# Reordering the loads and the early batches of a fused attention and gated-MLP kernel

## The chip, the cores and the metric

The kernel runs on one core of one Trainium2 chip. The metric is device time in microseconds (us). TensorE (PE) does matrix products, VectorE (DVE) and ScalarE (ACT) elementwise work, GpSimd (POOL) copies and the loads that cast, SyncE (SP) the output writes and the transposes done by DMA. Each engine runs its own instructions in program order and waits on semaphores for the others.

## The reference

Eight batches of eight heads, 576 positions, head size 64. A first attention packs k and v into 32 rows with p as queries; a second lets q attend to these 32 rows. The result, 4608 rows of 512, goes through a layer with h * cos(h) between two products.

```python
p_packed = sm_attn(p, k, v)            # p: 8 x 8 x 32 x 64
out = sm_attn(q, p_packed, p_packed)   # softmax with scale 1/8
x = out.transpose(0, 2, 1, 3).reshape(4608, 512)
h = x @ w_in                           # w_in: 512 x 2048
return (h * cos(h)) @ w_out            # w_out: 2048 x 512
```

Inputs and output are float32; the kernel computes in bf16 and accumulates in float32.

## The kernel before

**One batch** goes through these steps, each a helper function:

- `load(n, b)` brings k, q or v of a batch to SBUF with a cast to bf16, issued from POOL. `permute_v` rearranges v, on POOL or VectorE.
- k and q are transposed either by `pe_T` (24 PE transposes in three groups of eight, each group with one copy out of PSUM, L101 and L76) or by `xbar` (one DMA transpose on SP's queue, L92).
- `s1` (L123, L132): scores of p against k, and two exps on ScalarE into the tile a1. `recips`: reciprocals of its sums. a1 is transposed by `a1_pe` (12 PE transposes, two copies) or `a1_xbar` (DMA).
- `pp` (L162): the packed rows, copied out as ppT by two copies on VectorE and two on ScalarE.
- `ppw(b, n)` (L181): ppT times quarter n of w_in, giving PPW, with one cast out of PSUM by VectorE or ScalarE. The second attention is folded in this way, so that x is never formed.
- `s2` (L189): scores of q and two exps into a2u. `sums2` (L197, L199): sums over each head's 32 rows, and their logarithm. `normalise` (L205, L207): exp of the negated logarithm, and two VectorE instructions into a2n.
- `h_mm(b, fc)` for 16 chunks fc of 128 columns: four matmuls PPW by a2n (L220), the cosine on ScalarE (L224), the product h * cos(h) on VectorE into gT (L227), and a copy of the odd 64 rows into the tile joint on POOL (L231).
- `out_gen(b)`: gT times w_out (L270), 16 matmuls for each chunk c of 128 rows, a copy of the result to osb by VectorE or ScalarE in turn, and its write by SP. With 4 or 5 chunks a batch has 64 or 80 output matmuls.

**The order is written by hand.** `out_gen` is a generator; `fill(n)` puts the next n output matmuls of the batch before into TensorE's stream wherever it stands. So while slot s computes h of batch s, the output of batch s-1 fills TensorE. `set_filler` first uses up what is left and then starts on the next batch. `slot(s, ...)` runs the 16 chunks of `h_mm`, spreading the fillers evenly, with `pp`, `ppw`, `pack_p` and others put in at given chunks. What runs between two slots, from `ACT.preload_act_table_set` (ScalarE's table for exp and log; the cosine needs another) to `normalise`, is called the head of a slot here.

**Buffers.** TensorE writes to three PSUM tiles psA that are used strictly in turn: an allocation waits until whatever used the same buffer three allocations ago was read. Output matmuls have two tiles of their own (ot). There is one buffer each for kbf, qbf, vbf, kT and qT, so a load waits for the transpose of the batch before; v permuted has two.

**Start.** Batch 0 is handled with little to overlap, with `warm` matmuls on zeros in the gaps. Its cosine phase has no output to fill TensorE with. Loads stand in POOL's queue in this order: k, v, q of batch 0, the four quarters of w_in with the rest of p between, the four quarters of w_out, then k, v, q of batches 1 and 2.

```python
    set_filler(0)
    ACT.preload_act_table_set(EXP_SET)
    fill(4)
    pe_T("k", 1)
    fill(3)
    s1(1)
    permute_v(1, V)
    fill(8)
    a1_pe(1)
```

In the head of slot 1, 43 of batch 0's 64 output matmuls are placed, along with all of batch 1's attention and with k and s1 of batch 2.

Of the kernel before, what the change touches and what calls it, by code (L numbers as in the profile page):

```python
# [8 lines left out]
FP32 = mybir.dt.float32  # L9
# [6 lines left out]
def kernel(  # L16
# [55 lines left out]
    def copy(eng, out, in_):  # L72
        if eng is ACT:
            ACT.copy(out=out, in_=in_)  # L74
        else:
            eng.tensor_copy(out=out, in_=in_)  # L76
# [2 lines left out]
        return A.tile([128, 2, 512 if dt == FP32 else 1024], dt, name="psA", tag="A")  # L79

    def load(n, b):
        bf[n, b] = bf_pool.tile([TP, H, C * D], BF16, name=n + "bf", tag=n + "bf")
        G.dma_start(out=bf[n, b], in_=srcs[n][b].rearrange("h (p c) d -> p h (c d)", c=C))  # L83

    def permute_v(b, eng=G):
        vp[b] = vp_pool.tile([TP, C, H * D], BF16, name="vp", tag="vp")
        copy(eng, vp[b].rearrange("p c (h d) -> p c h d", h=H),
             bf["v", b].rearrange("p h (c d) -> p c h d", c=C))

    def xbar(n, b):  # L90
        t = xT[n, b] = att_pool.tile([128, H * 3, TP], BF16, name=n + "T", tag=n + "T")
        nc.sync.dma_start_transpose(out=t, in_=bf[n, b].rearrange("p h x -> p (h x)"))  # L92

    def pe_T(n, b, engs=(V, V, V)):
        t = xT[n, b] = att_pool.tile([128, H * 3, TP], BF16, name=n + "T", tag=n + "T")
        flat = bf[n, b].rearrange("p h x -> p (h x)")
        for i in range(3):
            ps = psa(BF16)
            for j in range(8):
                o = 8 * i + j  # L100
                nc.tensor.transpose(ps[:, 0, j * TP:(j + 1) * TP], flat[:, o * 128:(o + 1) * 128],  # L101
                                    ident[0:TP, 0:TP])
            copy(engs[i], t[:, 8 * i:8 * i + 8].rearrange("p a x -> p (a x)"),
                 ps[:, 0, 0:8 * TP])
# [69 lines left out]
    def ppw(b, n, eng=None):  # L174
        if b not in PPW:
            PPW[b] = ppw_pool.tile([128, 2, DF], BF16, name="PPW", tag="PPW")
        ps = psa()
        for x in range(4):
            for y in range(2):
                r = slice(64 * y, 64 * y + 64)  # L180
                nc.tensor.matmul(ps[32 * x:32 * x + 32, y, :], ppT[b % 2][r, 2 * x + y, :],  # L181
                                 w_in_bf[r, x, n * 512:(n + 1) * 512], start=True, stop=True)
        copy(eng or (V, ACT)[n % 2], PPW[b][:, :, n * 512:(n + 1) * 512], ps)

    def s2(b):
        a2u[b] = att_pool.tile([128, 2, S], BF16, name="a2u", tag="a2u")
        ps = scores(ppT[b % 2], xT["q", b])
        for y in range(2):
            ACT.activation(out=a2u[b][:, y].rearrange("p (e x) -> p e x", e=2),  # L189
                           in_=ps[y][:, :, 0:HS], func=AF.Exp, scale=rs1[b][:, y:y + 1])  # L190
# [46 lines left out]
    def pieces_of(b, c):  # L237
        ob = out[b * S:(b + 1) * S, :].rearrange("(p c) d -> c p d", c=C)
        if c == 4:
            o0 = out[(b - 1) * S:b * S, :].rearrange("(p c) d -> c p d", c=C)  # L240
            return [(0, 64, o0[5, 32:96]), (64, 128, ob[5, 32:96])]
        res, z = [], c * 128
        while z < c * 128 + 128:
            j, p0 = z // TP, z % TP
            n = min(TP - p0, c * 128 + 128 - z)
            res.append((z - c * 128, z - c * 128 + n, ob[2 * (j % 3) + j // 3, p0:p0 + n]))
            z += n
        return res

    def n_chunks(b):  # L250
        return 5 if b % 2 and b < B - 1 else 4
# [11 lines left out]
                q.dma_start(out=rows[:, cols], in_=osb[a:z, cols])  # L263

    def out_gen(b):
        for c in range(n_chunks(b)):
            ps = O.tile([128, DM], FP32, name="ot", tag="ot")
            for fc in range(NFC):
                w = joint[b // 2][:, fc, :] if c == 4 else gT[b][:, fc, c * 128:(c + 1) * 128]
                nc.tensor.matmul(ps, w, w_out_bf[:, fc, :], start=(fc == 0), stop=(fc == NFC - 1))  # L270
                if fc < NFC - 1:
                    yield
            osb = o_pool.tile([128, DM], FP32, name="osb")
            copy((V, ACT)[n_out[0] % 2], osb, ps)
            n_out[0] += 1
            for a, z, rows in pieces_of(b, c):
                nc.sync.dma_start(out=rows, in_=osb[a:z, :])
            yield

    filler = [None, 0]  # L280

    def set_filler(b):
        fill(1000)
        filler[0] = out_gen(b)
        filler[1] = 16 * n_chunks(b)
# [7 lines left out]
    def load_w_in(n):  # L293
        G.dma_start(out=w_in_bf[:, :, n * 512:(n + 1) * 512],
                    in_=moe_w_in.rearrange("(a p) n -> p a n", p=128)[:, :, n * 512:(n + 1) * 512])

    def load_w_out(n):
        G.dma_start(out=w_out_bf[:, n * 4:(n + 1) * 4, :],
                    in_=moe_w_out.rearrange("(a p) n -> p a n", p=128)[:, n * 4:(n + 1) * 4, :])

    def dup_p(a, b):
        for t in range(2):
            V.tensor_copy(out=p_bf[:, a:b, t, :], in_=p_raw[:, a:b, :])

    def warm(n):
        for _ in range(n):
            nc.tensor.matmul(wps, wz[:, 0:128], wz, start=True, stop=True)
# [3 lines left out]
    load("v", 0)  # L311
    make_identity(nc, ident)
    load("q", 0)
    load_w_in(0)
    load_w_in(1)
    G.dma_start(out=p_raw[:, 2:, :], in_=p_rows[:, 2:, :])
    load_w_in(2)
    load_w_in(3)
    for n in range(4):
        load_w_out(n)  # L320
    load("k", 1)
    load("v", 1)
    load("q", 1)
    load("k", 2)
    load("v", 2)
    load("q", 2)
    wz = const.tile([128, 512], BF16, name="wz")
    wps = O.tile([128, 512], FP32, name="wps", tag="ot")
    V.memset(wz, 0.0)
# [5 lines left out]
        V.memset(t[:, :, :, TP:128], 0.0)  # L335

    warm(7)
    dup_p(0, 2)
    pack_p(0, 1)
    warm(9)  # L340
    pe_T("k", 0, (V, ACT, V))
    s1(0)
    permute_v(0, V)
    warm(3)
    a1_pe(0)
    recips(0)
    pp(0)
    pe_T("q", 0, (V, ACT, V))
    s2(0)
    ppw(0, 0)  # L350
    sums2(0, 0)
    sums2(0, 1)
    normalise(0)
    warm(6)
    dup_p(2, 16)
    for fc in range(NFC):
        h_mm(0, fc)()
        if fc in (1, 4, 7):
            ppw(0, 1 + fc // 3)
        if fc == 10:  # L360
            pack_p(1, 3)

    set_filler(0)
    ACT.preload_act_table_set(EXP_SET)
    fill(4)
    pe_T("k", 1)
    fill(3)
    s1(1)
    permute_v(1, V)
    fill(8)  # L370
    a1_pe(1)
    recips(1)
    fill(4)
    pp(1)
    pe_T("q", 1)
    fill(3)
    ppw(1, 0)
    s2(1)
    fill(4)
    pe_T("k", 2)  # L380
    ppw(1, 1)
    fill(3)
    s1(2)
    fill(4)
    sums2(1, 0)
    fill(4)
    sums2(1, 1)
    normalise(1)
    fill(6)
    a1_pe(2)  # L390
    recips(2)
    load("k", 3)

    def slot(s, pieces, hooks, keep=5):
        left = filler[1] - keep
        for fc in range(NFC):
            rest = h_mm(s, fc)
            while pieces and pieces[0][0] == fc:
                pieces.pop(0)[1]()
            rest()  # L400
            while hooks and hooks[0][0] == fc:
                hooks.pop(0)[1]()
            done = left + keep - filler[1]
            fill((left * (fc + 1)) // NFC - done)

    def pw(b, n):
        return lambda: ppw(b, n)

    def pw2(b):
        fill(4)  # L410
        ppw(b, 0)
        ppw(b, 1)
        fill(4)

    def begin_loads(b):
        G.tensor_copy(out=gate, in_=xT["k", b][0:1, 0, 0:1])
        for n, i in (("v", b), ("q", b), ("k", b + 1)):
            load(n, i)

    permute_v(2)  # L420
    xbar("q", 2)
    xbar("k", 3)
    slot(1, [(1, pw(1, 2)), (4, pw(1, 3)), (7, lambda: pp(2)), (9, lambda: pack_p(3, B)),
             ], [(8, lambda: begin_loads(3)), (12, lambda: pw2(2))])

    for s in range(2, B):
        nxt = s + 1 < B
        fill(1000)
        set_filler(s - 1)
        ACT.preload_act_table_set(EXP_SET)  # L430
        if nxt:
            permute_v(s + 1)
        s2(s)
        ppw(s, 2, V)
        fill(8)
        if nxt:
            s1(s + 1)
            ppw(s, 3, V)
            xbar("q", s + 1)
            if s + 2 < B:  # L440
                xbar("k", s + 2)
            a1_xbar(s + 1)
            recips(s + 1)
            G.tensor_copy(out=gate, in_=a1T[s + 1][0:1, 0, 0, 0:1])  # L444
        else:
            ppw(s, 3, V)
        fill(4)
        sums2(s, 0)
        fill(5)
        sums2(s, 1)  # L450
        normalise(s)
        fill(13)
        for n, b in (("v", s + 2), ("q", s + 2), ("k", s + 3)):
            if b < B:
                load(n, b)
        pieces = [(5, lambda: pp(s + 1))] if nxt else []
        slot(s, pieces, [(9, lambda: pw2(s + 1))] if nxt else [])
    set_filler(B - 1)
    fill(1000)
    tail_chunk(B - 1, 4)  # L460
# [30 lines left out]
```

The softmax here doesn't subtract the row's maximum and nothing guards it: scores larger than these inputs give would overflow.

## Time and profile before

| | us |
|---|---|
| median of 8 runs | 262.55 |
| range of the runs | 261.05 to 263.7 |
| profiled execution, its own time | 261.05 |
| its span, first to last instruction | 259.2 |
| TensorE busy | 236.9 |
| VectorE busy | 165.8 |
| ScalarE busy | 167.0 |
| first cosine phase | 20.0 to 37.7 |
| head of slot 1 | 36.1 to 57.1 |
| slot 1, first to last product | 58.3 to 76.0 |
| slot 2 with its head | 76.0 to 104.2 |

In rows of the trace the columns are start, length, engine, line and operation, the tile written and those read, the count, and in brackets how long the engine had been idle and what ended that. In the rows of groups the count is followed by total busy time, mean ns of one, and the idle time before them. A busy TensorE includes the latency of its pipeline, so two matmuls in a row overlap in it. In a row of the windows each engine has its busy time and count; the last three columns are the clock that TensorE was granted, the share of the DMA engines, and GB/s.

### The profile page before, as it was taken

What the parts mean: (1) busy time and instruction counts of PE and PEld (TensorE: products, weight loads), DVE (VectorE), ACT (ScalarE), POOL (GpSimd) and SP (SyncE); (2) the same over time, 40 slices, a digit from 0 to 9 for tenths busy, and PEclk for the clock granted to TensorE, in tenths of its full rate; (3) what the DMA queues carried; (4) which work ended last, traced back from release to release, by engine and by line L of the source; (5) the groups of instructions that cost most, each with busy time, mean ns of one, the idle gap of its engine ahead of it and who ended that gap; (6) DMA issues with size and microseconds to landing.
All of it is one profiled execution on the core that took longest, in us unless ns stands there. A gap on an engine that the chain in (4) does not pass through costs nothing.

```text
span 259.2 us, 5031 instructions
## 1 busy us (share of the span) xinstructions
PE 236.9 (91%) x2004; PEld 132.9 (51%) x2037; DVE 165.8 (64%) x253; ACT 167.0 (64%) x270; POOL 53.7 (21%) x67
## 2 busy tenths in 40 slices
PE   8777769898989999999999998999999999999993
PEld 3443436554644656455545654565446564565452
DVE  2547876749875587568856675578755875687110
ACT  1377762497687657787787667777786576884000
POOL 8523002440422130504050305020310000000000
PEclk9997999999999999999999999999999999999999
DMA  6999999999499999699959993979193111121232
GB/s 95 203 226 206 206 205 200 206 200 177 71 204 206 192 138 218 117 196 159 210 105 194 166 215 87 170 158 206 57 148 88 40 43 40 40 52 46 66 83 81
DMA packets 62919, 37.09 MB, mean 143 GB/s; under 512 B 35520, under 2 KB 58304, under 8 KB 62896
## 3 DMA queue, kind: packets, MB, share of 16 engines
q0 software_dynamic: 23168, 18.81, 47.5%
q1 hardware_dynamic: 39568, 17.83, 33.1%
q8 instruction: 16, 0.26, 0.4%
q10 hardware_dynamic: 160, 0.13, 0.2%
q14 instruction: 7, 0.06, 0.1%
HBM read 37.22 MB, written 9.44 MB: 180 GB/s over the span
## 4 chain that ended last, share of the span: by engine, by line
PE 71%; DMA 13%; ACT 7%; DVE 4%; issue 2%; POOL 1%; DVEq 0%; POOLq 0%; ACTq 0%
PE ot L270 42%; PE psA L220 20%; DMA kbf<-in_k_dram 7%; DMA w_in_bf<-in_moe_w_in_dram 5%; PE psA L181 3%; DVE gT L227 2%; PE psA L162 2%; ACT cosT L224 1%; PE ot L259 1%; PE psA L123 1%; PE psA L197 1%; ACT a2u L189 1%; PE psA L101 1%; ACT L430 1%; ACT PPW L74 1%
## 5 line engine op out<-in xcount | busy, mean ns | idle before, releaser
L270 PE MATMUL ot<-w_out_bf,gT 128*128 128x512 bf16 x481 | 124.6, 379 | 1.7 <-issue 1.0
L227 DVE TENSOR_TENSOR gT<-psA,cosT 128x576 bf16<-128x576 f32 x128 | 94.0, 755 | 29.5 <-ACT cosT L224 28.0
L224 ACT ACTIVATE cosT<-psA 128x576 bf16<-128x576 f32 x128 | 81.8, 652 | 30.8 <-PE psA L220 28.2
L220 PE MATMUL psA<-a2n,PPW 128*128 128x288 bf16 x512 | 82.6, 289 | 7.3 <-DVE gT L227 3.4
L220 PEld LDWEIGHTS <-PPW 128*128 128x128 bf16 x512 | 50.4, 98 | 40.5 <-issue 12.4
L270 PEld LDWEIGHTS <-gT 128*128 128x128 bf16 x512 | 47.9, 98 | 44.6 <-issue 7.4
L76 DVE CAST PPW<-psA 128x1024 bf16<-128x1024 f32 x22 | 26.9, 1221 | 11.8 <-PE psA L181 11.8
L231 POOL COPY joint<-gT 128x512 bf16<-128x512 bf16 x16 | 9.8, 614 | 102.5 <-DVE gT L227 102.5
L76 DVE COPY osb<-ot 128x512 f32<-128x512 f32 (+1 forms) x19 | 12.8, 673 | 17.6 <-PE ot L270 14.6
L207 DVE SCALAR_TENSOR_TENSOR a2n<-a2u,r,lns 128x576 bf16<-128x576 bf16 x16 | 12.4, 815 | 16.0 <-ACT lns L205 16.0
L74 ACT COPY osb<-ot 128x512 f32<-128x512 f32 (+1 forms) x18 | 10.3, 575 | 17.9 <-PE ot L270 13.2
L76 POOL COPY vp<-vbf 96x3072 bf16<-96x3072 bf16 x6 | 16.5, 2749 | 0.6 <-DMA vbf<-in_v_dram 0.6
L199 ACT ACTIVATE lns<-psA 128x576 f32<-128x576 f32 x16 | 10.4, 654 | 5.7 <-PE psA L197 5.2
L132 ACT ACTIVATE a<-psA 128x576 bf16<-128x576 f32 x16 | 10.3, 649 | 5.8 <-PE psA L123 5.8
L74 ACT CAST PPW<-psA 128x1024 bf16<-128x1024 f32 x10 | 10.1, 1012 | 5.5 <-PE psA L181 5.5
L181 PE MATMUL psA<-w_in_bf,ppT 64*32 64x512 bf16 x256 | 12.1, 385 | 0.7 <-ACT a2u L189 0.4
L189 ACT ACTIVATE a2u<-psA,rs 128x576 bf16<-128x576 f32 x16 | 11.0, 738 | 2.6 <-PE psA L123 2.4
L270 PE MATMUL ot<-w_out_bf,joint 128*128 128x512 bf16 x48 | 12.3, 379 | 0.2
L172 ACT CAST ppT<-psA 64x128 bf16<-64x128 f32 x16 | 4.2, 260 | 11.2 <-DVE ppT L168 5.1
L83 POOL DMA_DIRECT2D kbf<-in_k_dram x8 | 6.3, 789 | 20.8 <-PE psA L101 17.2
L444 POOL COPY gate<-a1T 1x1 bf16<-1x1 bf16 x5 | 0.9, 182 | 45.8 <-DMA a1T<-a 45.8
L224 ACT ACT_TABLE_LOAD x8 | 10.3, 1283 | 0.1
(54 smaller groups left out, 149.4 us busy)
## 6 DMA issues: line engine op xcount, KB each, us to landing
kbf<-in_k_dram POOLq DMA_DIRECT2D x8, 576.0 KB, 11.2
vbf<-in_v_dram POOLq DMA_DIRECT2D x8, 576.0 KB, 6.2
qbf<-in_q_dram POOLq DMA_DIRECT2D x8, 576.0 KB, 9.2
out_dram<-osb SPq DMA_DIRECT2D x24, 192.0 KB, 2.8
out_dram<-osb SPq DMA_DIRECT2D x22, 128.0 KB, 2.4
w_in_bf<-in_moe_w_in_dram POOLq DMA_DIRECT2D x4, 512.0 KB, 15.1
w_out_bf<-in_moe_w_out_dram POOLq DMA_DIRECT2D x4, 512.0 KB, 19.9
out_dram<-osb SPq DMA_DIRECT2D x26, 64.0 KB, 2.1
```

What stands on the lines that cost most here:

```text
L74: ACT.copy(out=out, in_=in_)
L76: eng.tensor_copy(out=out, in_=in_)
L132: ACT.activation(out=a1[b % 2][:, y, :, 0:TP].rearrange("p (e m) x -> p e m x", e=2), in_=ps[y][:, :, 0:HS].rearrange("p e (m x) -> p e m ...
L181: nc.tensor.matmul(ps[32 * x:32 * x + 32, y, :], ppT[b % 2][r, 2 * x + y, :], w_in_bf[r, x, n * 512:(n + 1) * 512], start=True, stop=True)
L189: ACT.activation(out=a2u[b][:, y].rearrange("p (e x) -> p e x", e=2), in_=ps[y][:, :, 0:HS], func=AF.Exp, scale=rs1[b][:, y:y + 1])
L199: ACT.activation(out=lns[b][:, y].rearrange("p (e x) -> p e x", e=2), in_=ps[:, :, 0:HS], func=AF.Ln)
L207: V.scalar_tensor_tensor(out=a2n[b][:, y], in0=a2u[b][:, y], scalar=r1[b][:, y:y + 1], in1=lns[b][:, y], op0=ALU.mult, op1=ALU.mult)
L220: nc.tensor.matmul(ps[:, e, 0:HS], PPW[b][:, y, fc * 128:(fc + 1) * 128], a2n[b][:, y, e * HS:(e + 1) * HS], start=(y == 0), stop=(y == 1))
L224: ACT.activation(out=csv, in_=ps[:, :, 0:HS], func=AF.Sin, bias=PI_HALF)
L227: V.tensor_tensor(out=gT[b][:, fc, :].rearrange("p (e x) -> p e x", e=2), in0=ps[:, :, 0:HS], in1=csv, op=ALU.mult)
L231: G.tensor_copy(out=joint[b // 2][:, fc - 7:fc + 1, j0:j0 + 64], in_=gT[b][:, fc - 7:fc + 1, 512:576])
L270: nc.tensor.matmul(ps, w, w_out_bf[:, fc, :], start=(fc == 0), stop=(fc == NFC - 1))
```

## The change

- **Loads**: p's rest after w_in; then k, v and q of batch 1 ahead of w_out, v and q once batch 0's buffers are free; k2 and v2 after w_out. kbf and kT get two buffers.
- **VectorE to others**: p's casts (`dup_p(2, 16)`) and `permute_v(1)` to POOL; the third PPW quarter of batch 0 to ScalarE.
- **k1** is transposed after chunk 12 of the first cosine phase.
- **Head of slot 1**: only batch 1's attention, with 28 output matmuls; three PPW quarters cast by VectorE.
- **Output of batch 0**: chunks 0 and 1 in turn by quarters of w_out, then 2 and 3.
- **Slot 1** gets k2's and q2's transposes by TensorE (q2 came by DMA), the other things of batch 2 leave it; hooks run after the product of their chunk, in all slots.
- **Slot 2's head** takes s1, a1_pe and pp of batch 2 and s1 of batch 3, and all four PPW quarters of batch 2 are made in slot 2.

```diff
-        bf[n, b] = bf_pool.tile([TP, H, C * D], BF16, name=n + "bf", tag=n + "bf")
+        bf[n, b] = bf_pool.tile([TP, H, C * D], BF16, name=n + "bf", tag=n + "bf", bufs=2 if n == "k" else 1)
...
-        t = xT[n, b] = att_pool.tile([128, H * 3, TP], BF16, name=n + "T", tag=n + "T")
+        t = xT[n, b] = att_pool.tile([128, H * 3, TP], BF16, name=n + "T", tag=n + "T", bufs=2 if n == "k" else 1)
...
+        groups = [(0, 1), (2,), (3,)] if b == 0 else [(c,) for c in range(n_chunks(b))]
+        for grp in groups:
+            pss = {c: O.tile([128, DM], FP32, name="ot", tag="ot") for c in grp}
+            for f0 in range(0, NFC, 4):
+                for c in grp:
+                    for fc in range(f0, f0 + 4):
...
-    load_w_in(0)
-    load_w_in(1)
+    for n in range(4):
+        load_w_in(n)
     G.dma_start(out=p_raw[:, 2:, :], in_=p_rows[:, 2:, :])
-    load_w_in(2)
-    load_w_in(3)
-    for n in range(4):
-        load_w_out(n)
     load("k", 1)
-    load("v", 1)
-    load("q", 1)
-    load("k", 2)
-    load("v", 2)
-    load("q", 2)
...
     permute_v(0, V)
+    load("v", 1)
...
     pe_T("q", 0, (V, ACT, V))
+    load("q", 1)
+    for n in range(4):
+        load_w_out(n)
+    dup_p(2, 16, G)
+    load("k", 2)
+    permute_v(1, G)
+    load("v", 2)
     s2(0)
...
-    dup_p(2, 16)
     for fc in range(NFC):
         h_mm(0, fc)()
         if fc in (1, 4, 7):
-            ppw(0, 1 + fc // 3)
+            ppw(0, 1 + fc // 3, ACT)
         if fc == 10:
             pack_p(1, 3)
+        if fc == 12:
+            pe_T("k", 1)
...
+    s1(1)
+    pe_T("q", 1)
+    load("q", 2)
+    load("k", 3)
     fill(4)
...
     a1_pe(1)
     recips(1)
     fill(4)
     pp(1)
...
+    fill(6)
     s2(1)
...
+    ppw(1, 0, V)
     fill(4)
     sums2(1, 0)
...
     sums2(1, 1)
     normalise(1)
     fill(6)
+    ppw(1, 1, V)
+    ppw(1, 2, V)
+    fill(4)
+    slot(1, [(1, lambda: pe_T("k", 2)), (3, lambda: ppw(1, 3, ACT)), (5, lambda: pack_p(3, B)),
+             (7, lambda: permute_v(2)), (10, lambda: pe_T("q", 2)), (13, lambda: xbar("k", 3)),
+             (13, lambda: begin_loads(3))], 4)
+
+    fill(1000)
+    set_filler(1)
+    ACT.preload_act_table_set(EXP_SET)
+    s1(2)
+    fill(7)
     a1_pe(2)
     recips(2)
...
+    s1(3)
+    permute_v(3)
+    fill(4)
+    pp(2)
+    fill(6)
+    s2(2)
+    ppw(2, 0, V)
+    fill(8)
+    sums2(2, 0)
+    sums2(2, 1)
+    xbar("q", 3)
+    xbar("k", 4)
+    a1_xbar(3)
+    recips(3)
+    G.tensor_copy(out=gate, in_=a1T[3][0:1, 0, 0, 0:1])
+    normalise(2)
+    fill(8)
+    ppw(2, 1, V)
+    ppw(2, 2, V)
+    fill(8)
+    for n, b in (("v", 4), ("q", 4), ("k", 5)):
+        load(n, b)
+    slot(2, [(3, lambda: ppw(2, 3, ACT)), (6, lambda: pp(3)), (9, lambda: pw2(3))], 5)
```

More of the change, by code (lines that the diff above doesn't have):

```diff
@@ L90, in xbar @@
     def xbar(n, b):
-        t = xT[n, b] = att_pool.tile([128, H * 3, TP], BF16, name=n + "T", tag=n + "T")
+        t = xT[n, b] = att_pool.tile([128, H * 3, TP], BF16, name=n + "T", tag=n + "T", bufs=2 if n == "k" else 1)
         nc.sync.dma_start_transpose(out=t, in_=bf[n, b].rearrange("p h x -> p (h x)"))
     def pe_T(n, b, engs=(V, V, V)):
-        t = xT[n, b] = att_pool.tile([128, H * 3, TP], BF16, name=n + "T", tag=n + "T")
+        t = xT[n, b] = att_pool.tile([128, H * 3, TP], BF16, name=n + "T", tag=n + "T", bufs=2 if n == "k" else 1)
         flat = bf[n, b].rearrange("p h x -> p (h x)")
@@ L265, in out_gen @@
     def out_gen(b):
[L266 to L278, printed above, removed]
+        groups = [(0, 1), (2,), (3,)] if b == 0 else [(c,) for c in range(n_chunks(b))]
[4 more added lines that the diff above has]
+                    for fc in range(f0, f0 + 4):
+                        w = joint[b // 2][:, fc, :] if c == 4 else gT[b][:, fc, c * 128:(c + 1) * 128]
+                        nc.tensor.matmul(pss[c], w, w_out_bf[:, fc, :],
+                                         start=(fc == 0), stop=(fc == NFC - 1))
+                        if fc == NFC - 1:
+                            osb = o_pool.tile([128, DM], FP32, name="osb")
+                            copy((V, ACT)[n_out[0] % 2], osb, pss[c])
+                            n_out[0] += 1
+                            for a, z, rows in pieces_of(b, c):
+                                nc.sync.dma_start(out=rows, in_=osb[a:z, :])
+                        yield
     filler = [None, 0]
@@ L299, in load_w_out, with dup_p @@
                     in_=moe_w_out.rearrange("(a p) n -> p a n", p=128)[:, n * 4:(n + 1) * 4, :])
-    def dup_p(a, b):
+    def dup_p(a, b, eng):
         for t in range(2):
-            V.tensor_copy(out=p_bf[:, a:b, t, :], in_=p_raw[:, a:b, :])
+            eng.tensor_copy(out=p_bf[:, a:b, t, :], in_=p_raw[:, a:b, :])
     def warm(n):
@@ L337 @@
     warm(7)
-    dup_p(0, 2)
+    dup_p(0, 2, V)
     pack_p(0, 1)
@@ L358, with slot @@
         if fc in (1, 4, 7):
-            ppw(0, 1 + fc // 3)
+            ppw(0, 1 + fc // 3, ACT)
         if fc == 10:
             pack_p(1, 3)
[L363 to L394, printed above, removed]
+        if fc == 12:
+            pe_T("k", 1)
+    def slot(s, hooks, keep=0):
         left = filler[1] - keep
         for fc in range(NFC):
[L397 to L400, printed above, removed]
+            h_mm(s, fc)()
             while hooks and hooks[0][0] == fc:
@@ L404, in slot, with pw2 @@
             fill((left * (fc + 1)) // NFC - done)
-    def pw(b, n):
-        return lambda: ppw(b, n)
-    def pw2(b):
+    def pw2(b, n=0):
         fill(4)
-        ppw(b, 0)
-        ppw(b, 1)
+        ppw(b, n)
+        ppw(b, n + 1)
         fill(4)
@@ L418, in begin_loads @@
             load(n, i)
[L420 to L426, printed above, removed]
+    set_filler(0)
+    ACT.preload_act_table_set(EXP_SET)
[4 more added lines that the diff above has]
+    fill(4)
+    a1_pe(1)
+    recips(1)
+    fill(4)
+    pp(1)
+    fill(6)
+    s2(1)
+    ppw(1, 0, V)
+    fill(4)
+    sums2(1, 0)
+    sums2(1, 1)
+    normalise(1)
+    fill(6)
+    ppw(1, 1, V)
+    ppw(1, 2, V)
+    fill(4)
+    slot(1, [(1, lambda: pe_T("k", 2)), (3, lambda: ppw(1, 3, ACT)), (5, lambda: pack_p(3, B)),
[3 more added lines that the diff above has]
+    set_filler(1)
+    ACT.preload_act_table_set(EXP_SET)
+    s1(2)
+    fill(7)
+    a1_pe(2)
+    recips(2)
+    s1(3)
+    permute_v(3)
+    fill(4)
+    pp(2)
+    fill(6)
+    s2(2)
[16 more added lines that the diff above has]
+    slot(2, [(3, lambda: ppw(2, 3, ACT)), (6, lambda: pp(3)), (9, lambda: pw2(3))], 5)
+    for s in range(3, B):
         nxt = s + 1 < B
@@ L455 @@
                 load(n, b)
-        pieces = [(5, lambda: pp(s + 1))] if nxt else []
-        slot(s, pieces, [(9, lambda: pw2(s + 1))] if nxt else [])
+        slot(s, [(5, lambda: pp(s + 1)), (9, lambda: pw2(s + 1))] if nxt else [], 5)
     set_filler(B - 1)
```

## The prediction

> **What bounds the kernel now.** I read the page's busy shares first, then the table of windows cut at the stages, then the timeline of TensorE, VectorE and ScalarE over 16 to 108 us, last who waited for whom.
>
> ```profile
> PE 236.9 (91%) x2004; PEld 132.9 (51%) x2037; DVE 165.8 (64%) x253; ACT 167.0 (64%) x270; POOL 53.7 (21%) x67
> ...
> 20.00:36.00 16.00, 12.50 (x92) 7.30 (x92) 13.04 (x19) 11.87 (x18) 2.07 (x3) 0.89 1.25 206
> 36.00:39.00 3.00, 1.32 (x12) 0.62 (x11) 1.64 (x3) 2.22 (x3) 0.00 (x0) 1.00 1.32 204
> 39.00:58.30 19.30, 17.80 (x239) 10.65 (x239) 11.87 (x25) 10.40 (x20) 7.00 (x7) 1.00 1.30 202
> 58.30:76.20 17.90, 15.56 (x164) 9.12 (x162) 15.62 (x23) 13.14 (x21) 3.13 (x6) 1.00 0.86 146
> 76.20:105.00 28.80, 28.48 (x241) 15.68 (x238) 19.71 (x29) 21.25 (x35) 7.16 (x9) 1.00 1.05 181
> ```
>
> The columns after the length are PE, PEld, DVE, ACT and POOL busy. TensorE carries the whole, and from 76 us it is full (28.48 of 28.80). The change can win only where it is not: the first cosine phase (20 to 36), the wait for k1, the head of slot 1 (to 58) and slot 1 (to 76). There VectorE is close to the limit (15.62 of 17.90).
>
> ```profile
> 34.13 3.60 DVE L227 TENSOR_TENSOR gT<-psA,cosT 128x576 bf16<-128x576 f32 x5 [0.43 <-ACT cosT L224]
> ...
> 38.75 1.19 PE L101 MATMUL psA<-ident,kbf 96*128 96x96 bf16 x24 [1.63 <-DMA kbf<-in_k_dram]
> ...
> L76 DVE COPY kT<-psA 128x768 bf16<-128x768 bf16 x8 | 4.1, 553 | 5.2 <-PE psA L101 5.1
> L76 DVE CAST PPW<-psA 128x1024 bf16<-128x1024 f32 x22 | 26.9, 1221 | 11.8 <-PE psA L181 11.8
> L227 DVE TENSOR_TENSOR gT<-psA,cosT 128x576 bf16<-128x576 f32 x128 | 94.0, 755 | 29.5 <-ACT cosT L224 28.0
> ```
>
> The first row ends the cosine phase of batch 0 at 37.73; the second is the whole visible wait for k1, 1.63 us. The last three are the prices on VectorE: a third of a transposed k or q 0.55 (three in a row took 1.49), a quarter of PPW 1.22, a product gT 0.755.
>
> How much TensorE idles between 36.1 and the first s2 of slot 3 at 104.2, 68.1 us, I work out from start-to-start times, since busy time counts pipeline latency: 13 output matmuls took 2.97, less the last one's 0.38, so 0.216 each; 12 of L220 took 1.63, so 0.122 each. 144 output matmuls make 31.1, 128 of L220 15.7, and transposes, scores, sums, pp and ppw by their rows about 14.7: **61.5 busy, 6.6 idle**. That is the most that better order could bring.
>
> **What the Trainium skill says.** "TensorE: Matmul & The Clock Gate", section "Wait — 56ns, not 53.3ns?", gives 215.7 ns between warm 512-column matmuls; the trace agrees (0.216). Its section "What's actually happening" says that the array falls to half clock after an idle window and needs a busy one to recover; here the windows from 23 to 25 us show a granted 0.50 after the thinly filled start, though not a full stop. "DMA: Bandwidth & Descriptors", section "SWDGE vs HWDGE vs iDMA", says that a transfer that casts can be issued from GpSimd alone, so loads share one queue and its order decides; here w_out issued at 8.32 to 16.05 landed some 19.9 us later, and k1 behind it at 38.7. "SBUF — State Buffer", section "Who interferes with whom", says that a VectorE instruction with two SBUF inputs and a GpSimd one that reads SBUF block each other. The product has one input in PSUM, and it keeps 748 to 759 ns beside the joint copies in slot 1: I charge nothing for the copies moved to POOL.
>
> **The change, part by part**, against the profiled execution: span 259.2, its time 261.05; the median of the runs shown is 1.5 higher, and I add the same difference to it.
>
> *Loads.* Four w_out pieces ahead of k1 took 4 x 2.57 us (w_out 0 and 3 issued at 8.32 and 16.05 land near 28.3 and 36.0). Without them k1 lands near 28.4, v1 31, q1 34, w_out by quarters at 36.6, 39.2, 41.8, 44.3, k2 47, v2 50, q2 53, k3 56. On POOL, k2 now stands behind two casts (p, 896 elements; from the joint copy, 512 in 0.61, and the vp copy, 3072 in 2.75, I estimate 0.8 to 1.1 each), and v2 behind permute_v(1), 2.75; neither is late, as six earlier loads are still in flight. v1 and q1 issue behind permute_v(0) and pe_T(q0), done by 11.4 and 15. Cost: 0.
>
> *First cosine phase.* The p casts leave VectorE, but they ran 20.82 to 21.99 while the first cosine ended at 21.85: gain at most 0.15, taken as 0. The third PPW quarter goes from VectorE (1.22) to ScalarE (1.01): retiming the ring of three psA buffers, product 7 ends at 30.4 instead of 30.5 and product 10 at 33.4 as before: 0. Then k1's three copies, 1.49, stand between products 12 and 13, and product 13 waits for buffer 1, matmul 0.65 and cosine 0.65 behind the first copy, while two copies take 0.94: 0.45 more. TensorE's 1.19 for the transposes lies in its idle time. **+2.0**: the last product ends at 39.7, not 37.7.
>
> *Head of slot 1.* Gone: the 1.63 wait, the k1 transposes, pe_T(k2), s1(2), a1_pe(2), two ppw and 15 of 43 output matmuls. Left is a chain: EXP table 38.7 to 40.0, exps to 41.3, the third of pe_T(q1) needs the psA of the second exp, 41.9, four output matmuls 42.8, a1_pe and copies 44.4, pp and ppT 46.8, s2 and exps 48.7, sums and Ln 50.2, exps 51.4, normalise ending at 52.5. Before, it ended at 57.1. But behind normalise on VectorE now stand two PPW casts (2.44) and the first output copy (0.69), which is due with output matmul 28. The first product of slot 1 starts at **55.6 instead of 58.3**. The w_out quarters are needed at 42, 45, 48 and 51, each later than its landing. **-4.7** with the phase's +2.0 taken out; -2.7 up to here.
>
> *Slot 1.* Before: first product 58.28 to last 76.0, 17.7, made of 12.1 products, 4.5 other VectorE work and 1.1 idle. After: the other work is k2's and q2's copies (1.5 and 1.6; q2 came by DMA transpose), p's 0.8, one output copy 0.7: 4.6. Two pe_T break the ring, 0.45 each, and two output matmuls a chunk make TensorE's step 0.49 + 0.43 = 0.92 against 0.755, for which I add 0.5. Idle 2.5; 19.1 in all. **+1.4**: last product at 74.7 instead of 76.0.
>
> *Slot 2.* Before it took 76.0 to 104.2, 28.2, with TensorE full. After, it also holds s1(2) 0.44, a1_pe(2) 0.83, pp(2) 0.8 and two ppw 0.6, all on TensorE: +2.7. The head is now a chain of some 13 us (two rounds of exps, a1, pp, s2, sums) beside 45 output matmuls, 9.7, and 5 of other work; I add 0.7 idle, bounded by 0 and 3. **+3.4**: the first s2 of slot 3 at 106.3.
>
> *From slot 3 on* the same instructions run; pp's casts stand behind the product instead of ahead of it (0.6 us on an engine with slack): 0, bounds -0.3 and +0.3.
>
> The sum: +2.0 - 4.7 + 1.4 + 3.4 = **+2.1**. Profiled execution 263.2, median **264.6**. In short, idle taken from slot 1's head is paid back in the two phases that VectorE sets, and work is moved into the slot that was full.
>
> **Rivals.**
> *Output matmuls cover the chain (faster).* If the ring in slot 1 keeps VectorE busy, the last product comes at 55.6 + 16.7 = 72.3, and with k1's copies costing 1.5 in the phase and no idle in slot 2 the sum is 1.5 - 4.7 - 1.0 + 2.7 = -1.5: median 261.0. For it: before, four products ran in 2.97 in this slot. Against: TensorE's 0.92 a chunk. It decides when slot 1's last product comes before about 72.6.
> *The terms cancel (same).* Half of each doubt, idle 1.2 in slot 1 and 0.2 in slot 2, gives +0.3: 262.9.
> *a1T(3) comes late (slower still).* In slot 2, SP's transposes of q3, k4 and a1(3) start after s2(2), near 82, where s2 had read its q by 75.7 before; a1T landed 13.6 us after that (gate at 89.28), so now near 95.5, and pp(3), behind chunk 6, stands at about 95. TensorE waits in order, with output matmuls queued behind. At 0 to 2 us it gives up to 266.6; with the array at half clock for 3.4 us in the thin stretch around 40, as at 23 to 25, 1.5 more, 268.
> *k1 isn't there by chunk 12* (needed near 34): it would have to land 5.5 us later than worked out; the phase would stall, 265 to 268.
>
> **How the numbers follow.** About 1.3 us, 0.5%, can be told from no change. The forecast has 0.45, late a1T or a cold array 0.17, late k1 0.02: slower 0.64. Cancelling terms 0.22. Covered chain 0.14. The range goes from the covered chain's 261.0 to the cold case's 268.0.
>
> **What would show it.** Right: k1's transposes inside the cosine phase with no wait, its last product near 39.7; slot 1's first product near 55.6 behind two casts, VectorE over 85% busy up to a last product near 74.7; slot 2 some 31.6 long. Wrong: slot 1 ending by 72.5, or slot 2 under 30; or TensorE waiting for DMA anywhere between 36 and 105.

## The result: slower by 1.2%

| | before | changed |
|---|---|---|
| median of the runs, us | 262.47 (32 runs) | 265.3 (11 runs) |
| profiled execution, its own time | 261.05 | 265.11 |
| its span | 259.2 | 263.3 |

The ratio is 1.0118, 95% interval 1.0093 to 1.0144. The forecast was 264.6. Ratios and their intervals, here and below, are of fast executions alone, while the medians of a_k1_head and x1_sp_early each include two slow ones (without them 265.2 and 261.8).

First the page of the changed kernel: busy shares, and the clock that TensorE was granted in 40 slices of 6.6 us.

```profile
PE 238.9 (91%) x2029; PEld 134.2 (51%) x2061; DVE 164.5 (62%) x253; ACT 166.4 (63%) x270; POOL 58.0 (22%) x70
...
PEclk9999999979999999999999999999999999999999
```

TensorE gained only the transposes of q2, and it is idle for longer, 24.4 us of the span and not 22.3. The windows of the changed kernel, cut at its own stages (length, then busy us of PE, PEld, DVE, ACT, POOL; then clock, DMA share, GB/s), show where:

```profile
20.00:36.00 16.00, 12.23 (x116) 7.93 (x114) 11.55 (x19) 12.39 (x19) 7.57 (x8) 1.00 1.27 212
36.00:52.30 16.30, 13.52 (x165) 7.57 (x167) 10.94 (x19) 10.35 (x18) 2.94 (x5) 1.00 1.28 205
52.30:73.60 21.30, 19.19 (x161) 11.80 (x163) 15.99 (x25) 10.65 (x17) 4.15 (x4) 0.92 0.48 92
73.60:107.80 34.20, 31.16 (x307) 17.00 (x304) 22.31 (x34) 24.62 (x42) 8.30 (x11) 1.00 1.12 186
```

Slot 1 now has a mean clock of 0.92 and a VectorE that is 75% busy (15.99 of 21.30), where the forecast had over 85%. Slot 2, which was 28.48 busy in 28.80, has 3 us without a matmul. The marks of the forecast, from the timelines:

| | before | forecast | changed |
|---|---|---|---|
| last product of the first cosine phase ends | 37.73 | 39.7 | 37.92 |
| normalise of batch 1 ends | 57.11 | 52.5 | 49.48 |
| first product of slot 1 starts | 58.28 | 55.6 | 52.26 |
| last product of slot 1 ends | 76.0 | 74.7 | 73.60 |
| first s2 of slot 3 | 104.2 | 106.3 | 107.72 |
| from there to the end of the span | 155.0 | 155.0 | 155.6 |

The change is 6.0 us ahead at the start of slot 1, 2.4 ahead at its end, and 3.5 behind at the end of slot 2. VectorE of the changed kernel, from k1's copies to the first products of slot 1:

```profile
33.86 1.48 DVE L76 COPY kT<-psA 128x768 bf16<-128x768 bf16 x3
35.83 2.09 DVE L227 TENSOR_TENSOR gT<-psA,cosT 128x576 bf16<-128x576 f32 x3 [0.49 <-ACT cosT L224]
...
47.93 1.55 DVE L207 SCALAR_TENSOR_TENSOR a2n<-a2u,r,lns 128x576 bf16<-128x576 bf16 x2 [1.75 <-ACT lns L205]
49.39 2.35 DVE L76 CAST PPW<-psA 128x1024 bf16<-128x1024 f32 x2
51.66 0.68 DVE L76 COPY osb<-ot 128x512 f32<-128x512 f32 x1
52.26 1.41 DVE L227 TENSOR_TENSOR gT<-psA,cosT 128x576 bf16<-128x576 f32 x2
```

The steps are there as foreseen: the three copies and 0.49 for the refill of the psA ring, and two casts and an output copy between normalise and the first product, 2.8 us where 3.1 had been priced.

TensorE of the changed kernel in slots 1 and 2:

```profile
53.05 0.50 PE L101 MATMUL psA<-ident,kbf 96*128 96x96 bf16 x8 [0.76 <-DVE gT L227]
...
54.66 1.17 PE L220 MATMUL psA<-a2n,PPW 128*128 128x288 bf16 x4
56.47 1.17 PE L220 MATMUL psA<-a2n,PPW 128*128 128x288 bf16 x4
58.40 0.65 PE L220 MATMUL psA<-a2n,PPW 128*128 128x288 bf16 x4
...
70.11 0.59 PE L273 MATMUL ot<-w_out_bf,gT 128*128 128x512 bf16 x2
70.55 0.65 PE L220 MATMUL psA<-a2n,PPW 128*128 128x288 bf16 x4
71.04 0.59 PE L273 MATMUL ot<-w_out_bf,gT 128*128 128x512 bf16 x2
...
76.14 1.17 PE L154 MATMUL psA<-ident,a 128*96 128x128 bf16 x12 [0.74 <-ACT a L132]
...
95.31 0.86 PE L162 MATMUL psA<-a1T,vp 96*128 96x64 bf16 x24 [1.18 <-DMA a1T<-a]
...
103.56 0.65 PE L220 MATMUL psA<-a2n,PPW 128*128 128x288 bf16 x4 [0.55 <-DVE gT L227]
```

The same four matmuls take 1.17 at 54 to 58 and 0.65 afterwards: the array ran at half clock there, from 54.31 to 57.73. Away from that spell, the two pe_T and the other steps put in, slot 1 goes at TensorE's pace: two output matmuls and four of L220 follow without a break, and so each product starts 0.92 after the last, the step that was worked out, with VectorE waiting 0.16 for the cosine:

```profile
70.08 0.76 DVE L227 TENSOR_TENSOR gT<-psA,cosT 128x576 bf16<-128x576 f32 x1 [0.16 <-ACT cosT L224]
71.00 0.76 DVE L227 TENSOR_TENSOR gT<-psA,cosT 128x576 bf16<-128x576 f32 x1 [0.17 <-ACT cosT L224]
```

In slot 2, a1_pe waits 0.74 for batch 2's exps, pp(3) waits 1.18 for the DMA transpose of a1, and one L220 waits 0.55 for a product. No row shows TensorE waiting for w_out, k1, v1, k2 or q2. The 1.18 is a wait for a DMA all the same, which the prediction had named as a sign of being wrong anywhere between 36 and 105.

### The profile page after: what moved, and what is told of

It reads as the page before. It is cut to its first block, busy times and chain, and to the rows that moved or that the text cites. A ratio compares the mean times of both kernels' runs of the same rounds, so it can differ in the third digit from the quotient of the medians.

```text
span 263.3 us, 5077 instructions
## 1 busy us (share of the span) xinstructions
PE 238.9 (91%) x2029; PEld 134.2 (51%) x2061; DVE 164.5 (62%) x253; ACT 166.4 (63%) x270; POOL 58.0 (22%) x70
## 4 chain that ended last, share of the span: by engine, by line
PE 68%; ACT 10%; DVE 8%; DMA 7%; issue 3%; SPq 1%; POOL 1%; ACTq 0%; DVEq 0%; POOLq 0%
PE ot L273 40%; PE psA L220 19%; DVE gT L227 5%; DMA qbf<-in_q_dram 4%; ACT cosT L224 3%; DMA a1T<-a 3%; PE psA L181 3%; PE psA L162 2%; ACT a2u L189 2%; PE psA L123 1%; PE ot L259 1%; SPq L92 1%; DVE a2n L207 1%; PE psA L197 1%; PE psA L101 1%
## 5 line engine op out<-in xcount | busy, mean ns | idle before, releaser
L227 DVE TENSOR_TENSOR gT<-psA,cosT 128x576 bf16<-128x576 f32 x128 | 93.6, 755 | 35.6 <-ACT cosT L224 34.3
L224 ACT ACTIVATE cosT<-psA 128x576 bf16<-128x576 f32 x128 | 81.1, 652 | 32.9 <-PE psA L220 31.8
L220 PE MATMUL psA<-a2n,PPW 128*128 128x288 bf16 x512 | 82.5, 288 | 5.1 <-DVE gT L227 3.3
L220 PEld LDWEIGHTS <-PPW 128*128 128x128 bf16 x512 | 50.3, 98 | 39.0 <-issue 9.4
L76 DVE COPY osb<-ot 128x512 f32<-128x512 f32 (+1 forms) x19 | 12.8, 673 | 17.6 <-PE ot L273 14.6
L76 POOL COPY vp<-vbf 96x3072 bf16<-96x3072 bf16 x7 | 19.3, 2750 | 6.9 <-DMA vbf<-in_v_dram 6.9
L172 ACT CAST ppT<-psA 64x128 bf16<-64x128 f32 x16 | 4.2, 260 | 15.8 <-DVE ppT L168 10.1
L205 ACT ACTIVATE lns<-lns 128x576 f32<-128x576 f32 x16 | 10.0, 680 | 0.0
L310 PE MATMUL wps<-wz 128*128 128x512 bf16 x23 | 8.2, 511 | 1.4 <-DVE wz L323 1.2
## 6 DMA issues: line engine op xcount, KB each, us to landing
w_out_bf<-in_moe_w_out_dram POOLq DMA_DIRECT2D x4, 512.0 KB, 20.8
```

Of the source, the lines that this page charges most:

```text
L205: ACT.activation(out=lns[b][:, y], in_=lns[b][:, y], func=AF.Exp, scale=-1.0)
L220: nc.tensor.matmul(ps[:, e, 0:HS], PPW[b][:, y, fc * 128:(fc + 1) * 128], a2n[b][:, y, e * HS:(e + 1) * HS], start=(y == 0), stop=(y == 1))
L224: ACT.activation(out=csv, in_=ps[:, :, 0:HS], func=AF.Sin, bias=PI_HALF)
L227: V.tensor_tensor(out=gT[b][:, fc, :].rearrange("p (e x) -> p e x", e=2), in0=ps[:, :, 0:HS], in1=csv, op=ALU.mult)
```

## The experiments

The theory: the loads do what they should, slot 1 is set by VectorE and the ring of three psA buffers, and slot 2 pays for the work moved into it and for a late a1T. (Of slot 1 the rows above bear it out where copies are put in; between them TensorE sets the pace.) In the names, a_ and x are runs of the changed kernel with an edit, and b_ runs of the kernel before. Each run is timed against the kernel before on the same chip. "Slot 1" is from first to last product, "slot 2" from there to the first s2 of slot 3.

| run | median, us | ratio to before (95%) | slot 1 | slot 2 |
|---|---|---|---|---|
| changed kernel | 265.30 | 1.0118 (1.0093 to 1.0144) | 21.3 | 34.1 |
| a_q2_xbar | 265.57 | 1.0121 (1.0087 to 1.0154) | 18.9 | 37.2 |
| a_a1T_first | 264.13 | 1.0064 (1.0042 to 1.0085) | 21.4 | 32.9 |
| a_k1_head | 265.64 | 1.0109 (1.0076 to 1.0143) | 19.7 | 34.3 |
| a_casts | 263.45 | 1.0059 (1.0034 to 1.0083) | 20.8 | 34.3 |
| x1_sp_early | 261.91 | 0.9988 (0.9954 to 1.0022) | 19.0 | 32.9 |
| x1_no_s1_2 | 259.57 | 0.9913 (0.9884 to 0.9943) | 17.4 | 30.5 |
| x2_sp_casts | 260.54 | 0.9939 (0.9917 to 0.9961) | 18.4 | 33.4 |
| x3_k1_head | 260.32 | 0.9933 (0.9909 to 0.9957) | 18.4 | 33.5 |
| b_k1_early | 261.72 | 0.9972 (0.9951 to 0.9992) | 17.7 | 28.2 |
| b_loads_quarters | 261.58 | 0.9969 (0.9945 to 0.9993) | 17.7 | 28.2 |
| b_lq_k1_first | 259.96 | 0.9920 (0.9895 to 0.9945) | 17.7 | 28.2 |

### q2 by DMA transpose again (a_q2_xbar)

```diff
-             (7, lambda: permute_v(2)), (10, lambda: pe_T("q", 2)), (13, lambda: xbar("k", 3)),
+             (3, lambda: xbar("q", 2)), ... (7, lambda: permute_v(2)), (13, lambda: xbar("k", 3)),
```

> The changed kernel with q2 transposed by DMA on SP's queue (put in at chunk 3 of slot 1) instead of by TensorE and VectorE at chunk 10. Theory (slot 1 is set by VectorE and the ring of three psA buffers): without the three copies (1.48) and the ring's refill at 65 to 69 us, the last product of slot 1 comes some 2.3 us sooner after the first (21.3 to about 19.0), and the time falls by about 2 us against the changed kernel. Rival (slot 2's chain of SP transposes behind s2(2) and the output matmuls decide, slot 1 only waits differently): slot 1 is shorter but slot 2 longer by as much, time within 0.7 us of the changed kernel.

Both halves came true at once: slot 1 fell by 2.4, as the theory said, and the time did not move. Who TensorE waited for in slots 1 and 2 of this run, and SP's transposes there:

```profile
PE psA L162 <- DMA a1T<-a: 2.5, 1, 2.5
```

```profile
83.02 3.71 SPq L92 DMA_TRANSPOSE qT<-qbf  x1
86.83 3.67 SPq L92 DMA_TRANSPOSE kT<-kbf  x1
90.59 1.46 SPq L146 DMA_TRANSPOSE a1T<-a  x1
```

s2(2) came 2.3 us sooner than in the changed kernel (78.3, not 80.6), but the chain of q3, k4 and a1 started at 83.02 where it had started at 83.30, since q3's load had not landed and SP waited 2.7 for it. That load waits for k3's transpose, which stayed at 67.3 behind an output write. So pp(3) waited 2.5 instead of 1.2, and after that wait the clock fell to 0.50, from 95.7 to 99.1. Slot 2 is 3.1 longer (37.2, not 34.1): the wait makes 1.3 of it, and the other 1.7 is about what such a spell costs in slot 1, 1.6 (see a_k1_head). Time won ahead of a wait with an anchor of its own went into the wait and what came behind it.

### a1 transposed first (a_a1T_first)

```diff
+    a1_xbar(3)
     xbar("q", 3)
     xbar("k", 4)
-    a1_xbar(3)
     recips(3)
-    G.tensor_copy(out=gate, in_=a1T[3][0:1, 0, 0, 0:1])
+    G.tensor_copy(out=gate, in_=xT["k", 4][0:1, 0, 0:1])
```

> The changed kernel with the DMA transpose of a1(3) ahead of those of q3 and k4 on SP in slot 2, and the loads of batch 4 released by k4's transpose instead of a1's. Theory (pp(3) of slot 2 waits for a1T, with TensorE's stream behind it): the 1.2 us wait of TensorE at 94 to 95 goes, and the ring need not be refilled; time 1.2 to 1.8 us below the changed kernel. Rival (TensorE in slot 2 has slack behind VectorE, so the wait is hidden, or the next wait ends at the same time): within 0.5 us.

SP's transposes in this run:

```profile
82.23 2.37 SPq L146 DMA_TRANSPOSE a1T<-a  x1
84.71 5.57 SPq L92 DMA_TRANSPOSE qT<-qbf  x1
90.37 3.02 SPq L92 DMA_TRANSPOSE kT<-kbf  x1
```

The wait is gone, slot 2 is 1.2 shorter, and the median is 1.2 below the changed kernel's: the wait was on the path.

### k1 in the head instead of the phase (a_k1_head)

```diff
-        if fc == 12:
-            pe_T("k", 1)
...
     ACT.preload_act_table_set(EXP_SET)
+    pe_T("k", 1)
     s1(1)
```

> The changed kernel with k1's transposes taken out of the first cosine phase and put at the head of slot 1, ahead of s1(1). Theory (three copies and the refill of the ring cost the phase 1.9 us, and in the head they stand behind the EXP table load that ScalarE needs anyway): last product of the phase at 35.9 instead of 37.8, first product of slot 1 at 51.5 to 52.3, time within 0.8 us of the changed kernel. Rival (moving k1 into the phase is the part that pays): first product of slot 1 later by 1.5 us or more, time 1.5 us above.

The phase's last product ended at 36.35, and the first product of slot 1 started at 52.48, 0.2 later than in the changed kernel. The place of k1's transposes is worth nothing: what the phase gives back, the head takes. This profile had no spell at half clock. Its own time, 263.94, is below most runs of this kernel (263.6 to 268.4), so its median doesn't tell what the spell costs; slot 1 of the profile does, below. The windows over slot 1 in this run, for the row at 52.30 above:

```profile
52.50:72.20 19.70, 17.58 (x162) 11.28 (x163) 16.01 (x25) 10.54 (x17) 4.09 (x4) 1.00 0.52 99
```

With the same instructions at full clock slot 1 took 19.7 instead of 21.3: the spell costs 1.6. x1_no_s1_2 below shows the same once more: up to the end of slot 1 its program is that of x1_sp_early, its profile has the spell earlier, in the head, and the slot took 17.4 instead of 19.0.

### Casts out of the first product's way (a_casts)

```diff
     sums2(1, 1)
+    ppw(1, 1, V)
     normalise(1)
-    fill(6)
-    ppw(1, 1, V)
-    ppw(1, 2, V)
-    fill(4)
-    slot(1, [(1, lambda: pe_T("k", 2)), (3, lambda: ppw(1, 3, ACT)), ...
+    fill(10)
+    slot(1, [(1, lambda: pe_T("k", 2)), (2, lambda: ppw(1, 2, ACT)), (5, lambda: ppw(1, 3, ACT)), ...
```

> The changed kernel with the two PPW casts that stand behind normalise in slot 1's head moved: quarter 1 ahead of normalise on VectorE, quarter 2 to ScalarE at chunk 2, quarter 3 at chunk 5. Theory (the two casts, 2.35 us on VectorE, hold up the first product of slot 1, and the idle TensorE there brings the half-clock spell at 54 to 58): first product at about 50.6 instead of 52.3, no spell at 54 to 58, last product 2 to 3 us sooner, but since slot 2's a1T chain does not move, only 0 to 1 us of it reaches the end. Rival (the three psA buffers and ScalarE, which takes the cast, set slot 1): last product of slot 1 within 1 us of 73.6.

The first product started at 50.98, no spell showed, and the last product ended 1.8 sooner: less than the 2 to 3 expected. More of it reached the end than expected, 1.6 us of the span and 1.9 of the median, because here the whole slot moved: k3's DMA transpose went out at 65.4 instead of 67.2 and a1's at 89.8 instead of 91.5, and pp(3) waited 1.4.

### SP's order mended (x1_sp_early), and then the casts (x2_sp_casts)

```diff
-             (10, lambda: pe_T("q", 2)), (13, lambda: xbar("k", 3)), (13, lambda: begin_loads(3))
+             (3, lambda: xbar("q", 2)), (5, lambda: xbar("k", 3)), (9, lambda: begin_loads(3))
...
+    a1_xbar(3)
     xbar("q", 3)
     xbar("k", 4)
-    a1_xbar(3)
```

> The changed kernel with q2 transposed by DMA at chunk 3 as in the earlier run, k3's DMA transpose at chunk 5 instead of 13, batch 3's loads at chunk 9 instead of 13, and a1(3) transposed ahead of q3 and k4. Theory (what q2's DMA transpose won in slot 1 was lost in slot 2 to pp(3)'s wait for a1T, since the SP chain there hangs on the loads and not on slot 1): slot 1 stays at 19, slot 2 falls from 37.2 to 32 to 33, no wait for a1T; time 3 to 3.8 us below the changed kernel, about 261.7. Rival (slot 2 is set by TensorE and its own chain, which lengthen whatever comes sooner): slot 2 at 34 or more, time no better than 264.

Four edits at once, so their shares are not told apart, but the sum is as forecast: slot 1 at 19.0 and slot 2 at 32.9, and the median 3.4 below the changed kernel. It still had a half-clock spell at 54 to 58.

> The two runs above together, and in slot 2 the casts of quarters 1 and 2 moved in the same way. Theory (waits of slot 1 and slot 2 add up): slot 1's last product near 69, first s2 of slot 3 near 101.5; time 1.5 to 2 us below the run with the SP order alone, about 260, so below the kernel before. Rival (TensorE's own work, which the change left the same up to slot 3, is the limit by then): within 0.7 us of the run with the SP order alone.

In slot 1 the edit is that of a_casts, in slot 2 the same for batch 2. The casts brought 1.4 more: last product of slot 1 at 69.2, no spell in the profile, 0.6% below the kernel before. Slot 2 did not get shorter by its own moved casts (33.4 against 32.9).

> The changed kernel with the SP order and the casts moved, and k1's transposes taken from the first cosine phase to the head of slot 1. Theory (as in the earlier run with k1 in the head, the phase ends 1.6 us sooner and the head takes as much longer): within 0.5 us of the run without this edit, 260.5. Rival (k1 in the phase is worth its place once slot 1 no longer waits): 0.8 us or more above it.

The edit is that of a_k1_head, on top of x2_sp_casts: 260.32 against 260.54. Again its place is worth nothing that can be measured.

### The price of batch 2's s1 in slot 2 (x1_no_s1_2)

```diff
-    s1(2)
+    a1T[2], r1[2], rs1[2] = a1T[1], r1[1], rs1[1]
     fill(7)
-    a1_pe(2)
-    recips(2)
```

> The changed kernel with the SP order alone moved, and batch 2's p scores, exps, transposes of a1 and reciprocals left out (batch 1's are used in their place). Theory (this work, put into a slot that was full, is paid there in full: matmuls 0.44 and 0.83, and TensorE's wait for the exps 0.7): slot 2 with its head shorter by about 2 us, 32.9 to 31, time 1.7 to 2.3 us below the run with the work. Rival (it lies beside output matmuls and VectorE's products and costs nothing in slot 2): within 0.5 us.

Slot 2 fell from 32.9 to 30.5, and the time by 2.3 in the medians and 2.0 by the ratios: matmuls of 1.3 us and a head wait of 0.7 that had been moved there are paid in full, and some 0.4 more.

### The loads alone, on the kernel before (b_k1_early, b_loads_quarters, b_lq_k1_first)

```diff
+    load("k", 1)
     for n in range(4):
         load_w_out(n)
-    load("k", 1)
```

> The kernel before with one edit: k1 is loaded ahead of the four quarters of w_out. Theory (the wait for k1 is a real loss at the head of slot 1, and a quarter of w_out is not needed until later): TensorE's 1.63 us wait goes, time 1.2 to 1.7 us below the kernel before. Rival (the first cosine phase of that profile ran with three us at half clock, the wait only took up what the phase lost, or v1 and w_out now come late): within 0.5 us of the kernel before.

Half of what was expected. VectorE and TensorE of this run show where the wait went:

```profile
42.14 0.96 DVE L76 COPY vp<-vbf 96x3072 bf16<-96x3072 bf16 x1 [3.39 <-DMA vbf<-in_v_dram]
43.02 1.01 DVE L76 COPY a1T<-psA 96x768 bf16<-96x768 bf16 x2
```

```profile
44.08 0.86 PE L162 MATMUL psA<-a1T,vp 96*128 96x64 bf16 x24 [1.49 <-DVE a1T L76]
```

v1, still behind w_out, is late next. `permute_v(1)` waits for it on VectorE, the copies of a1T stand behind it in order, and TensorE waits 1.49 for them. This profile also shows half clock from 45.3 to 48.7, right behind the wait, which the kernel before does not. So all three loads of batch 1 were moved, and batch 0's output taken by quarters of w_out:

> The kernel before with the load part of the change alone: k1, v1 and q1 ahead of w_out, batch 0's output by quarters of w_out; all of the batches' work stays where it was. Theory (loading k1 alone moved the wait to v1, 1.49 us, so the load part pays once v1 and q1 come along; what costs in the change is the work moved, not the loads): no DMA wait of TensorE between 36 and 60 us, first product of slot 1 some 2 us sooner, time 1.3 to 2.2 us below the kernel before. Rival (w_out now comes too late for the output matmuls that fill the head, whatever the order): TensorE waits for w_out at 36 to 45 us, time within 0.6 us of the kernel before or above it.

Neither of the two answers alone: the wait for v1 was gone, and another of nearly the same length was left, for the first quarter of w_out. TensorE of this run, and then of the one after it, where k1's transposes go ahead of those output matmuls:

```profile
37.30 1.02 PE L273 MATMUL ot<-w_out_bf,gT 128*128 128x512 bf16 x3 [1.52 <-DMA w_out_bf<-in_moe_w_out_dram]
38.16 1.19 PE L101 MATMUL psA<-ident,kbf 96*128 96x96 bf16 x24
```

```profile
36.67 0.50 PE L101 MATMUL psA<-ident,kbf 96*128 96x96 bf16 x8 [0.35 <-DVE gT L227]
37.34 0.50 PE L101 MATMUL psA<-ident,kbf 96*128 96x96 bf16 x8 [0.17 <-DVE gT L227]
37.68 1.68 PE L273 MATMUL ot<-w_out_bf,gT 128*128 128x512 bf16 x7
```

```diff
-    fill(4)
     pe_T("k", 1)
-    fill(3)
+    fill(7)
```

> The kernel before with the load part alone, as run earlier, and k1's transposes ahead of the first output matmuls of the head instead of behind four of them. Theory (in the earlier run the wait had moved from k1 to the first quarter of w_out, 1.52 us at 37.3; put behind k1's transposes it is covered): no DMA wait at 36 to 40, 0.8 to 1.5 us below the run with the load part alone, about 260.4. Rival (w_out is late by as much at the next four output matmuls): within 0.5 us of it.

No DMA wait of TensorE is left in the head, and no kernel of the study that computes the whole has a lower median: 259.96, 0.8% below the kernel before, with slots 1 and 2 as long as before (17.7 and 28.2). The two profiles show 0.8 of the 1.6 us between the medians of the last two runs (first product of slot 1 at 57.68 and 56.89).

So the load part of the change is a gain, 0.3% as it stood and 0.8% with k1's transposes ahead. The rest, in the order that the change gave it, is a loss that hides the gain; in the order of x3_k1_head the whole is at 0.9933 with an interval that overlaps that of the loads alone (0.9920), so the moved work neither pays nor costs anything that is clear there.

## Why the prediction was right, by its steps

The direction was right and the size of the sum near, and so was the idea that what the head gains is paid back in slots 1 and 2. Most of the single terms were off, in both directions.

**Loads: right.** k1, v1, q1 and all quarters of w_out landed in the order worked out, each 1.0 to 1.4 us later (k1 at 29.75, the first quarter of w_out at 37.78, the last at 45.39), and were there when needed. On POOL the two casts of p took 1.81 together, inside the estimate.

**First cosine phase, +2.0: measured +0.2.** The price of k1's copies was right: the phase took 16.2 in the changed kernel and 14.4 with them in the head, 1.8. What failed was the retiming of the rest, which I took from rows in which the array stood at half clock for 3.4 of the sixteen us, as this window of the kernel before shows:

```profile
23.00:24.00 1.00, 1.00 (x6) 0.63 (x5) 0.31 (x1) 0.44 (x2) 0.41 (x1) 0.50 1.23 206
```

In the three b_ runs, whose phase has no such spell, the old instructions took 14.8 instead of 15.8. So about 1.0 was a spell that the changed kernel didn't have there. The old order took 14.8 and the new one, in a_k1_head, 14.4: some 0.4 goes with casting the third quarter on ScalarE and p on POOL, which I had put at nothing. The 1.0 was luck of a profile, not a gain of the kernel: before, TensorE had to wait for k1 behind the spell in any case, and with its 261.05 this execution is as fast as those at full clock throughout (below).

**Head of slot 1, -4.7: measured -6.2.** From the phase's end to normalise it took 11.6, not 12.8; the two casts and the copy behind it 2.8, not 3.1. The chain's hops were added up too generously.

**Slot 1, +1.4: measured +3.6.** 1.6 of the difference is the half-clock spell, by the same slot without it, which at 19.7 is near the 19.1 of the forecast. The price of pe_T(q2) was right: without it, slot 1 is 2.4 shorter with the spell still there, against 1.6 of copies, 0.45 for the ring and part of 0.5 for TensorE's step.

**Slot 2, +3.4: measured +5.9.** This was the largest miss. The work of s1(2) with its wait costs 2.4, against 1.3 of matmuls and the 0.7 of idle that I had added. Too small was the idle: TensorE stands for 3.0 us of the slot, where it stood for 0.4 before. Of it, 1.2 is pp(3)'s wait for a1T, which stood among the rivals and is shown on the path by a_a1T_first, 0.7 the wait for batch 2's exps, and 0.55 the wait for a product at 103.6, put at nothing. Some 0.6 of the 5.9 is in neither the priced matmuls nor the idle, and no run here splits it.

**From slot 3 on, 0: measured +0.6**, outside my bounds. It comes as 0.3 between the first and last product of slot 3 and again of slot 5, while slots 4 and 6 take as long as before. Every profile with the changed hooks has 155.6 to 155.8 for this stretch and every one without them 155.0 to 155.1, so it belongs to the change; which wait it is stays open.

**The rivals.** The late a1T was not instead of the forecast but on top of it: worked out to land near 95.5, it released pp(3) at 95.3, with TensorE there at 94.1. The covered chain failed for the reason given, TensorE's 0.92 a chunk. Its turning point, a last product before 72.6, did not hold, since slot 2 cost more than forecast: a_k1_head, a_casts and a_q2_xbar had it at 72.2, 71.8 and 71.3 and were still slower by 0.6 to 1.2%. x1_sp_early, with 71.5 and a slot 2 that is 1.2 shorter, came out even. The cold array came true, but at 54 to 58 and not at 40.

That 2.1 us of forecast stand beside 2.8 of the medians is in part luck, twice over. Terms cancel: the phase and the head came out 3.3 better than worked out, slots 1 and 2 together 4.7 worse, and the stretch from slot 3 on 0.6 worse, so that the profiles differ by 4.1. And I had added 1.5 us for the distance from the profiled execution to the median, since that of the kernel before was the fastest of its runs; in the changed kernel the distance is 0.2. Not tried: the output by quarters without the loads, and the copies moved to POOL each by itself.

## What to carry to other kernels

Moving a late transfer ahead shows what is late next, here v1 after k1 and the first quarter of w_out after v1; follow it until no wait is left before judging the move. Work taken out of a thin stage is a gain only if it doesn't go into a full one, and time won ahead of a wait is kept only if what ends the wait moves as well. Look for half clock in a profile before retiming its rows. Test the parts of a change apart: here the loads alone won 0.3%, 0.8% with one more step, and the whole lost 1.2%.

## What the runs showed of the hardware

TensorE fell to half clock without ever stopping for long. Windows of the changed kernel:

```profile
50.00:52.00 2.00, 1.22 (x11) 0.67 (x10) 2.00 (x3) 1.27 (x2) 0.00 (x0) 1.00 1.31 203
52.00:53.00 1.00, 0.29 (x7) 0.19 (x5) 1.00 (x3) 0.00 (x0) 0.00 (x0) 1.00 1.31 203
53.00:54.00 1.00, 0.78 (x15) 0.67 (x15) 1.00 (x3) 0.00 (x0) 0.00 (x0) 1.00 1.32 205
...
55.00:56.00 1.00, 1.00 (x5) 0.51 (x4) 0.06 (x1) 0.63 (x2) 0.00 (x0) 0.50 0.67 187
```

Four us in which it was busy for 2.3, with no stop longer than 0.76, were followed by 3.4 us at 0.50, worth 1.6 us in slot 1. The Trainium skill, "TensorE: Matmul & The Clock Gate", section "A second HAM failure mode: psum-queue depth-cycling", tells of a kernel in which short idle moments between groups of matmuls, as it cycles through the PSUM banks, sent the clock back and forth between half and full. What came before this spell is of that kind: short waits for the next psA buffer, held up by VectorE.

Up to 250 us the thirteen profiles show nine such spells, and each lasted 3.41 us. A thin stretch makes one possible and not certain. The spell at 54 to 58 showed in the changed kernel, a_q2_xbar, a_a1T_first and x1_sp_early, and not in a_k1_head and x1_no_s1_2, which have the same gap. The 3.4 us up to the start of the spell at 22.55 in the profile of before are thin (TensorE 49% busy). Eleven others have a stretch just as thin at that place (48 to 49%, ending at 22.4 to 23.2), and none of them has a spell there.

The scatter between executions goes with the spells, too. One of 3.4 us at half clock takes 0.0065 off the mean clock of a span of 263 us. Of the thirteen executions of the changed kernel whose clock is on record, the two at 0.997 took 263.7 and 264.0, the nine at 0.991 to 0.994 265.1 to 265.4, and the two at 0.985 and 0.986 267.0 and 266.6. Of the 63 of the kernel before that stand beside a_casts, the sixteen at 1.000 took 261.1 to 261.6, and the eight at 0.984 or less 263.9 to 264.6; in between, at 0.987 to 0.993, times from 261.0 to 263.5 occur, so a spell can also cost next to nothing, as the one ahead of the wait for k1 did. With the least half clock the change is thus still some 2.5 us slower, so its loss does not rest on the spells.
